# One more fold of the odd rows of a sequence DFT: half-length products for seven of eight sequences

## The chip, the cores and the metric

One core of a Trainium2 chip. The metric is the time of one execution in device microseconds (us). The kernel before the change takes 1992.16 us, the median of 4 runs that share their rounds with the changed kernel (1991.02 to 1994.47). "PE" is TensorE, "DVE" VectorE, "ACT" ScalarE, "POOL" GpSimd.

## The reference

```python
def _attn_ref(x):                       # x: 8 x 3008 x 256, fp32
    X = np.fft.fft(x, axis=1)
    X = np.fft.fft(X, axis=2)
    return X.real.astype(np.float32)

def _moe_ref(x, w_in, w_out):           # x: 24064 x 256; w_in 256 x 2048; w_out 2048 x 256
    h = x @ w_in
    r = np.maximum(h, 0.0)
    return ((r * r) @ w_out).astype(np.float32)
```

The output of the first part, reshaped to 24064 x 256, is the input of the second.

## The kernel before

The DFT over the 3008 rows of a sequence is done as products with cosine and sine tables. Symmetries cut it down: row n is folded with S - n and S/2 +- n, so 753 rows remain (S = 3008), and these fall into classes. Class 3 holds the 376 odd n; it is by far the longest product. The classes are cut into tiles of at most 128 rows: class 0 has one of 95 rows, class 1 one of 94, class 2 two of 128 and 60, class 3 three of 128, 128 and 120.

The feature DFT is merged into the input weights (`G1`, `G2`), and the two weight products run over 6 blocks of 251 output rows with 8 steps each, 48 steps a sequence. While PE works on sequence b, the engines fold sequence b + 1 and PE does its DFT in between; small "pieces" of that work are released by `between()`, twice a step, according to a pace.

```python
def group(kp, which):                      # one of 4 groups of a sequence: even or odd k, cosine or sine part
    ...
    def product(ps, c):
        ts = [t for t in range(NT) if TILES[t][0] == c]
        for t in ts:
            rows = TILES[t][3]
            w = we[t] if b is None else folded[b, t, which % 2]
            w = w[0:rows, kp]
            ...
            nc.tensor.matmul(ps, w, tab[0:rows, kp, PLACE[t]:PLACE[t] + NC[kp][c]],
                             start=t == ts[0], stop=t == ts[-1])

    def even_n():                          # classes 0, 1, 2: 95, 94, then 128 and 60 rows
        ...
        for c, at, nk in ((0, 0, n2), (1, n2, n2), (2, 2 * n2, n1)):
            product(st["ps"][:, at:at + nk], c)
        nc.scalar.copy(a[:, 0:n2], st["ps"][:, 0:n2])
    ...
    def odd_n():                           # class 3: 128, 128, 120 rows, 377 or 376 columns
        st["odd"] = psd.tile([P, 512], F32, name="pd", tag="d")[0:n, 0:n0]
        product(st["odd"], 3)
```

```python
def between():
    nonlocal spent
    if i < 2 * NJ:                         # NJ = 8 steps a block
        return
    spent -= pace
    while side and spent <= 0:
        t, f = side.pop(0)                 # t: weight of the piece, f: emits its instructions
        f()
        spent += t
```

The stationary operand of a DFT product is the folded data (up to 128 rows x 128 columns); the table streams past it. Each fp32 product in the source appears in the trace as two passes, each with a weight load.

## Time and profile before

| | before |
|---|---|
| median, this comparison | 1992.16 us |
| PE busy | 1957.8 us, 98% |
| DVE / ACT / POOL busy | 70% / 45% / 58% |
| distance of one DFT to the next (steady sequences) | 237.77 us |
| one even-n group, first pass to next product | 1.48 us |
| one odd-n group, first pass to next product | 1.90 us |

A busy engine is read here from the page's shares, the critical path from the chain that ended last, and the cost of a product from the *starts* of passes in the timeline. The recorded length of a pass is longer than what it costs: a pass of 189 columns is recorded with 0.32 us, but the next one starts 0.16 us after it. The prediction shows those lines. The distance of one DFT to the next is read off the chain in order of time, where the first even-n group of each sequence stands:

```profile
467.16 1.28 PE pd L349 x8
...
704.93 1.28 PE pd L349 x8
```

704.93 - 467.16 = 237.77 us. All six steady sequences agree to a few hundredths of a us.

### The profile page before, as it was taken

To read this page: it belongs to the slowest core of one execution; us is meant where nothing else is said; L and a number is where in the kernel's file an instruction comes from. 1 tells how busy PE (TensorE), PEld (TensorE's weight loads), DVE (VectorE), ACT (ScalarE), POOL (GpSimd) and SP (SyncE) were. 2 spreads that over 40 slices of the span, in tenths; PEclk is the share of its full clock that TensorE was granted. 3 is DMA by queue.
4 is the path that set the end of the run, shared out by engine and by line. 5 is a ranking of instruction groups with operands and counts; after the bars stand their busy time and mean duration, and the time that the engine had idled before them with its cause. 6 is when DMAs were issued, how large, how long until landed. Compare 5 with 4: busy or idle time off the path is not lost.

```text
span 1991.9 us, 27283 instructions
## 1 busy us (share of the span) xinstructions
PE 1957.8 (98%) x9104; PEld 1701.1 (85%) x9104; DVE 1391.3 (70%) x3492; ACT 896.2 (45%) x973; POOL 1158.8 (58%) x1695
## 2 busy tenths in 40 slices
PE   6999999999999999999999999999999999999998
PEld 3788888888888888888888888888888888888887
DVE  7889867776578765787558875677756876555554
ACT  1654444444444444444344443444444444445443
POOL 0037646666566655666557665666656675566664
PEclk8999999999999999999999999999999999999999
DMA  6331101110011111111011110121002100100100
GB/s 190 110 39 47 38 11 37 47 27 22 18 46 32 40 19 27 27 41 39 11 32 32 39 30 11 32 51 29 22 11 52 32 11 16 32 11 11 22 11 21
DMA packets 144687, 68.49 MB, mean 34 GB/s; under 512 B 128440, under 2 KB 135547, under 8 KB 144546
## 3 DMA queue, kind: packets, MB, share of 16 engines
q1 hardware_dynamic: 143470, 66.24, 14.1%
q8 instruction: 71, 1.16, 0.2%
q14 instruction: 70, 0.57, 0.1%
q10 hardware_dynamic: 1076, 0.52, 0.1%
HBM read 42.03 MB, written 24.68 MB: 33 GB/s over the span
## 4 chain that ended last, share of the span: by engine, by line
PE 94%; DVE 2%; DMA 1%; ACT 1%; SPq 0%; issue 0%; DVEq 0%; ACTq 0%
PE ph L412 16%; PE ph L413 16%; PE mA L465 16%; PE mC L465 16%; PE mB L465 16%; PE mD L465 8%; PE pd L349 5%; DMA xt<-in_x_dram 1%; DMA raw<-in_moe_w_in_dram 1%; DVE he L415 0%; DVE g L418 0%; ACT g L427 0%; ACT g L428 0%; SPq L163 0%; DVE g L417 0%
## 5 line engine op out<-in xcount | busy, mean ns | idle before, releaser
L427 ACT ACTIVATE g<-g 128x1004 f32<-128x1004 f32 (+1 forms) x384 | 399.6, 1041 | 894.3 <-DVE g L418 511.1
L415 DVE SCALAR_TENSOR_TENSOR he<-Et,gE,ph 128x251 f32<-128x251 f32 (+1 forms) x768 | 361.8, 471 | 476.6 <-PE ph L413 475.1
L435 POOL TENSOR_TENSOR s<-g 128x251 f32<-128x251 f32 (+1 forms) x376 | 248.9, 662 | 739.3 <-ACT g L428 668.1
L412 PE MATMUL ph<-Pt,G 128*128 128x251 f32 (+1 forms) x1536 | 453.4, 376 | 4.5 <-ACT G L237 3.4
L413 PE MATMUL ph<-Qt,G 127*128 127x251 f32 (+1 forms) x1536 | 451.3, 374 | 0.2 <-DVE Qt L362 0.2
L428 ACT ACTIVATE g<-g 128x1004 f32<-128x1004 f32 (+1 forms) x384 | 399.3, 1040 | 12.1
L465 PE MATMUL mC<-s,wsum 128*128 128x251 f32 (+1 forms) x1504 | 381.3, 374 | 0.0
L465 PE MATMUL mA<-g,wout 128*128 128x251 f32 (+1 forms) x1504 | 381.0, 375 | 0.0
L417 DVE TENSOR_TENSOR g<-he,ph 128x251 f32<-128x251 f32 (+1 forms) x768 | 320.6, 417 | 55.6 <-POOL s L437 0.5
L412 PEld LDWEIGHTS ph<-Pt,G 128*128 128x128 f32 x1536 | 287.2, 189 | 48.7 <-ACT G L237 4.0
L413 PEld LDWEIGHTS ph<-Qt,G 127*128 127x128 f32 x1536 | 291.1, 190 | 36.4 <-DVE Qt L362 0.6
L465 PEld LDWEIGHTS mA<-g,wout 128*128 128x128 f32 x1504 | 282.5, 189 | 41.7 <-issue 2.9
L465 PEld LDWEIGHTS mC<-s,wsum 128*128 128x128 f32 x1504 | 285.5, 190 | 34.5
L418 DVE TENSOR_TENSOR g<-he,ph 128x251 f32<-128x251 f32 (+1 forms) x768 | 314.2, 409 | 0.0
L436 POOL TENSOR_TENSOR s<-s,g 128x251 f32<-128x251 f32 (+1 forms) x376 | 282.0, 750 | 29.4
L437 POOL TENSOR_TENSOR s<-g 128x251 f32<-128x251 f32 (+1 forms) x376 | 291.4, 775 | 0.0
L438 POOL TENSOR_TENSOR s<-g,s 128x251 f32<-128x251 f32 (+1 forms) x376 | 246.0, 654 | 0.0
L465 PE MATMUL mB<-g,wsum 128*128 128x251 f32 (+1 forms) x752 | 220.5, 374 | 0.0
L465 PE MATMUL mD<-s,wout 128*128 128x251 f32 (+1 forms) x752 | 220.3, 374 | 0.0
L465 PE MATMUL mB<-s,wout 128*128 128x251 f32 (+1 forms) x752 | 219.9, 374 | 0.0
L465 PEld LDWEIGHTS mB<-g,wsum 128*128 128x128 f32 x752 | 142.6, 190 | 17.4
L465 PEld LDWEIGHTS mD<-s,wout 128*128 128x128 f32 x752 | 141.9, 189 | 17.7
(85 smaller groups left out, 1264.3 us busy)
## 6 DMA issues: line engine op xcount, KB each, us to landing
out_dram<-os SPq DMA_DIRECT2D x376, 56.0 KB
xt<-in_x_dram SPq DMA_DIRECT2D x24, 512.0 KB
xt<-in_x_dram SPq DMA_DIRECT2D x16, 384.0 KB
Et<-e_dram SPq DMA_DIRECT2D x7, 752.5 KB
out_dram<-os SPq DMA_DIRECT2D x288, 6.8 KB
raw<-in_moe_w_in_dram SPq DMA_DIRECT2D x16, 256.0 KB
raw<-in_moe_w_out_dram SPq DMA_DIRECT2D x16, 256.0 KB
xt<-in_x_dram SPq DMA_DIRECT2D x8, 480.0 KB
```

The source lines that it names most:

```text
L412: nc.tensor.matmul(hP, G1[:, fs], pt[:, ks], start=True, stop=True)
L413: nc.tensor.matmul(hQ, G2[:, fs], qt[:, ks], start=True, stop=True)
L415: nc.vector.scalar_tensor_tensor(out=t, in0=et[:, ks], scalar=gE[:, fc:fc + 1], in1=hP, op0=ALU.mult, op1=ALU.add)
L417: tt(out=g[:, h, 0, 0:n], in0=t, in1=hQ, op=ALU.add)
L418: tt(out=g[:, h, 1, 0:n][:, ::-1], in0=t, in1=hQ, op=ALU.subtract)
L427: act(v, v, AF.Relu)
L428: act(v, v, AF.Square)
L435: gt(out=s1, in0=g21, in1=g22, op=ALU.add)
L436: gt(out=s2, in0=s1, in1=g11, op=ALU.subtract)
L437: gt(out=s3, in0=g11, in1=g21, op=ALU.subtract)
L438: gt(out=s4, in0=g12, in1=s2, op=ALU.subtract)
L465: nc.tensor.matmul(acc[nm][:, i, 0:n], w, v[:, 0:n], start=j == 0 and i == 0, stop=j == NJ - 1, skip_group_check=True)
```

## The change

The 376 odd rows are folded once more, n with S/4 - n, into 188 rows for each of two data sets. For even k both sets multiply the same table, one its even and one its odd columns, and each yields every second output column (`ps[:, part:n0:2]`). For odd k one set multiplies the cosine table and the other the sine table, and the output columns are sums and differences of the two (`join_odd`). Per odd-n group PE then streams 4 products of 189 or 188 columns instead of 3 of 377 or 376. For each of the two new tiles the fold needs rows in reverse order (a lane shuffle on DVE), two more additions, a rotation by a twiddle factor per row (ACT and DVE), and tables whose even and odd columns are sorted apart, done once on ACT. Also, the preparation of sequence 1 begins eight steps earlier at half pace. Sequence 0 keeps the old form.

```diff
             def odd_n():
-                st["odd"] = psd.tile([P, 512], F32, name="pd", tag="d")[0:n, 0:n0]
-                product(st["odd"], 3)
+                ps = psd.tile([P, 512], F32, name="pd", tag="d")[0:n]
+                st["odd"] = ps[:, 0:n0]
+                if b == 0 or b is None and kp:
+                    return product(ps[:, 0:n0], 3)
+                nq = (n0 + 2) // 2 if kp else (n0 + 1) // 2
+                for part in range(2):
+                    ...                    # tab, o, to = where this part reads and writes
+                    for i, (rows, pair) in enumerate(((P, (ODD0, ODD0 + 1)), (REST, (ODD0 + 2, NT)))):
+                        nc.tensor.matmul(to, folded[b, pair[other]][0:rows, kp, PART[which]][:, 0:n],
+                                         columns(tab, ODD0 + i, o)[0:rows], start=i == 0, stop=i == 1)
+                if kp:
+                    st["cos"] = hp.tile([P, nq], F32, name="oc", tag="oc", bufs=1)[0:n]
+                    nc.scalar.copy(st["cos"], ps[:, 0:nq])
+                    st["sin"] = ps[:, nq:2 * nq]
...                                        # fold pieces of the odd tiles
+        def f_even():
+            v, w, a = st["v"][rows, 0], st["w"][rows, 0], st["f0"][rows]
+            tt(out=v, in0=a, in1=w, op=ALU.add)
+            tt(out=w, in0=a, in1=w, op=ALU.subtract)
+            sine(spare("f1", "f1"), st["w"], (0, 1))
+            sine(spare("f2", "f0"), st["v"], (1, 0))
...
-        return [(0.7, f_s), (0.7, f_d), (0.5, f_sc), (0.4, f_dc), (0.6, f_p), (0.6, f_q)]
+        ops = [(0.7, f_s), (0.7, f_d), (0.6, f_sc), (0.4, f_dc), (0.5, f_p), (0.5, f_q)]
...
+        return ops + [(0.7, f_turn), (0.9, f_even), (1.0, f_odd)]
...
-        if i < 2 * NJ:
+        if i < NJ:
             return
-        spent -= pace
+        spent -= pace / 2 if i < 2 * NJ else pace
```

Here `P` is 128 and `REST` is 60: 188 = 128 + 60.

More of the change, by code (lines that the diff above doesn't have):

```diff
@@ L112 @@
     fp = ctx.enter_context(tc.tile_pool(name="fp", bufs=2))
-    wp = ctx.enter_context(tc.tile_pool(name="wp", bufs=NT))
+    wp = ctx.enter_context(tc.tile_pool(name="wp", bufs=NT + 1))
     pq = ctx.enter_context(tc.tile_pool(name="pq", bufs=2))
@@ L129 @@
     xt = {}
-    def load_x(b, t):
-        _, r0, step, rows = TILES[t]
+    ODD0 = NT - 3
+    HALF = S // 16
+    REST = HALF - P
+    ODD = [[(0, 0, P)],
+           [(p, 2 * HALF - p - R, R) for p in range(0, P, R)],
+           [(0, P, H // 2)] + [(H // 2 + p, 2 * HALF - P - p - R, R) for p in range(0, H // 2, R)]]
+    assert H == P and REST <= H // 2 and TILES[ODD0][0] == 3 and TILES[ODD0 + 1][1] == TILES[ODD0][1] + P
+    def load_x(b, t):
+        c, r0, step, rows = TILES[t]
+        if b and c == 3:
+            xt[b, t] = xp.tile([P, 4, D], F32, name="xt", tag="x")
+            for p, first, count in ODD[t - ODD0]:
+                nc.sync.dma_start(out=xt[b, t][p:p + count], in_=x[b, S // 8 + 1 + first:S // 8 + 1 + first + count])
+            return
         while rows % 15 and rows % 16 and r0 + step * rows < NROW:
@@ L263, with make_turn, part_table, columns @@
     PQE = {}
+    PART = (slice(0, H + 1), slice(H + 1, D))
+    REVERSE = list(range(R - 1, -1, -1))
+    turn = const.tile([P, 3, 2], F32, name="turn")
+    def make_turn():
+        for i in range(2):
+            for a, tab in enumerate((cosT, sinT, sinT)):
+                nc.scalar.mul(turn[:, a, i:i + 1], tab[:, 1, PLACE[ODD0 + i]:PLACE[ODD0 + i] + 1], -1.0 if a == 2 else 1.0)
+    def part_table(tab, t):
+        nk = NC[0][3]
+        v = tab[:, 0, PLACE[t]:PLACE[t] + nk]
+        a = op.tile([P, nk], F32, name="tp", tag="os")
+        nc.scalar.copy(a, v)
+        nc.scalar.copy(v[:, 0:(nk + 1) // 2], a[:, 0::2])
+        nc.scalar.copy(v[:, (nk + 1) // 2:], a[:, 1::2])
+    def columns(tab, t, part):
+        nk, at = NC[0][3], PLACE[t]
+        if t == NT - 1:
+            return tab[:, 0, at + part:at + nk:2]
+        nq = (nk + 1) // 2
+        return tab[:, 0, at + part * nq:at + (nk if part else nq)]
     NE = B - 1
@@ L266 @@
     e_dram = dp.tile([NE, NKT], F32, name="e_dram")
-    e_rows = const.tile([NE, NKT], F32, name="e_rows")
     def load_column(t):
@@ L285, in fold @@
     def fold(b, t):
-        r = slice(0, TILES[t][3])
+        odd = b > 0 and t >= ODD0
+        r = slice(0, P if odd else TILES[t][3])
         st = {}
@@ L312, in f_dc, with w_of @@
             tt(out=new(fp, "dc", [P, 2, H - 1])[r], in0=d[r, :, 1:H], in1=d[r, :, D - 1:H:-1], op=ALU.subtract)
+        def w_of(t):
+            if (b, t) not in folded:
+                folded[b, t] = wp.tile([P, 2, D], F32, name="w", tag="w")
+            return folded[b, t]
         def f_p():
-            sc, wP = st["sc"], new(wp, "wP", [P, 2, H + 1])
+            sc, w = st["sc"], w_of(t)
             for kp in range(2):
-                tt(out=wP[r, kp], in0=sc[r, 0], in1=sc[r, 1], op=ALU.subtract if kp else ALU.add)
@@ L318, in f_p @@
-            folded[b, t, 0] = wP
+                tt(out=w[r, kp, PART[0]], in0=sc[r, 0], in1=sc[r, 1], op=ALU.subtract if kp else ALU.add)
         def f_q():
-            dc, wQ = st["dc"], new(wp, "wQ", [P, 2, H - 1])
+            dc, w = st["dc"], w_of(t)
             for kp in range(2):
-                tt(out=wQ[r, kp], in0=dc[r, 0], in1=dc[r, 1], op=ALU.add if kp else ALU.subtract)
-            folded[b, t, 1] = wQ
-        return [(0.7, f_s), (0.7, f_d), (0.5, f_sc), (0.4, f_dc), (0.6, f_p), (0.6, f_q)]
+                tt(out=w[r, kp, PART[1]], in0=dc[r, 0], in1=dc[r, 1], op=ALU.add if kp else ALU.subtract)
@@ new lines, in fold, with f_turn @@
+        ops = [(0.7, f_s), (0.7, f_d), (0.6, f_sc), (0.4, f_dc), (0.5, f_p), (0.5, f_q)]
+        if not odd or t == ODD0:
+            return ops
+        i = t - ODD0 - 1
+        rows = slice(0, TILES[ODD0 + i][3] if i == 0 else REST)
+        def f_turn():
+            w = w_of(t)
+            if i == 0:
+                st["v"], st["w"] = w_of(ODD0), w
+                nc.vector.stream_shuffle(w, w, REVERSE)
+            else:
+                st["v"], st["w"] = w, w_of(NT)
+                nc.vector.stream_shuffle(st["w"][0:H // 2], w[H // 2:P], REVERSE)
+            spare("f0", "f0")
+            nc.scalar.copy(st["f0"][rows], st["v"][rows, 0])
@@ new lines, in spare, with sine @@
+        def spare(nm, tag):
+            st[nm] = fp.tile([P, D], F32, name=nm, tag=tag, bufs=1)
+            return st[nm]
+        def sine(to, src, signs):
+            for part, a in zip(PART, signs):
+                nc.scalar.mul(to[rows, part], src[rows, 1, part], turn[rows, 1 + a, i:i + 1])
+        def f_even():
[4 more added lines that the diff above has]
+            sine(spare("f2", "f0"), st["v"], (1, 0))
@@ L328, in dft_ops, with f_odd @@
+        def f_odd():
+            for nm, u in (("f1", "v"), ("f2", "w")):
+                u = st[u][rows, 1]
+                nc.vector.scalar_tensor_tensor(out=u, in0=u, scalar=turn[rows, 0, i:i + 1], in1=st[nm][rows],
+                                               op0=ALU.mult, op1=ALU.add)
+        return ops + [(0.7, f_turn), (0.9, f_even), (1.0, f_odd)]
     def dft_ops(b):
@@ L345, in product @@
                     rows = TILES[t][3]
-                    w = we[t] if b is None else folded[b, t, which % 2]
-                    w = w[0:rows, kp]
+                    w = (we[t] if b is None else folded[b, t][:, :, PART[which % 2]])[0:rows, kp]
                     w = w[:, H:H + 1].to_broadcast([rows, n]) if which == 2 and b is not None else w[:, 0:n]
@@ L378, in odd_n @@
             def odd_n():
-                st["odd"] = psd.tile([P, 512], F32, name="pd", tag="d")[0:n, 0:n0]
-                product(st["odd"], 3)
+                ps = psd.tile([P, 512], F32, name="pd", tag="d")[0:n]
[5 more added lines that the diff above has]
+                    if kp:
+                        tab, o = (cosT, sinT)[part], 0
+                        to = ps[:, part * nq:part * nq + nq]
+                        other = part != which
+                    else:
+                        tab, o = (cosT, sinT)[which % 2], part
+                        to = ps[:, part:n0:2]
+                        other = part != which
+                    if b is None:
+                        for t in range(ODD0, NT):
+                            rows, at = TILES[t][3], PLACE[t]
+                            nc.tensor.matmul(to, we[t][0:rows, kp], columns(tab, t, part)[0:rows],
+                                             start=t == ODD0, stop=t == NT - 1)
+                        continue
+                    for i, (rows, pair) in enumerate(((P, (ODD0, ODD0 + 1)), (REST, (ODD0 + 2, NT)))):
+                        nc.tensor.matmul(to, folded[b, pair[other]][0:rows, kp, PART[which]][:, 0:n],
+                                         columns(tab, ODD0 + i, o)[0:rows], start=i == 0, stop=i == 1)
@@ new lines, in odd_n, with join_odd @@
+                if kp:
+                    st["cos"] = hp.tile([P, nq], F32, name="oc", tag="oc", bufs=1)[0:n]
+                    nc.scalar.copy(st["cos"], ps[:, 0:nq])
+                    st["sin"] = ps[:, nq:2 * nq]
+            def join_odd():
+                a, ps = st["cos"], st["sin"]
+                nq = a.shape[-1]
+                st["odd"] = o = hp.tile([P, NC[1][3]], F32, name="do", tag="do", bufs=1)[0:n, 0:n0]
+                tt(out=o[:, 0::2], in0=a[:, 0:nq - 1], in1=ps[:, 0:nq - 1], op=ALU.add)
+                if which == 1:
+                    tt(out=o[:, 1::2], in0=ps[:, 1:nq], in1=a[:, 1:nq], op=ALU.subtract)
+                else:
+                    tt(out=o[:, 1::2], in0=a[:, 1:nq], in1=ps[:, 1:nq], op=ALU.subtract)
@@ L382, in join_1 @@
             def join_1():
-                dst = e_rows if b is None else PQE[b][which]
+                dst = PQE[1][2][0:n] if b is None else PQE[b][which]
                 nh = S // 8
@@ L386, in join_1 @@
                      st["odd"])
-            return [(0.5, even_n), (0.5, join_4), (0.7, join_2), (0.0, odd_n), (1.2, join_1)]
+            ops = [(0.1, even_n), (0.5, join_4), (0.7, join_2), (0.1, odd_n), (1.1, join_1)]
+            if b and kp:
+                ops.insert(4, (0.7, join_odd))
+            return ops
         ops = [] if b is None else [(0.0, start)]
@@ L394, in dft_ops @@
         if b is None:
-            ops.append((0.0, lambda: nc.sync.dma_start(out=e_dram[:, :], in_=e_rows)))
+            ops.append((0.0, lambda: nc.sync.dma_start(out=e_dram[:, :], in_=PQE[1][2][0:NE])))
         return ops
@@ L630 @@
                 load_column(i - NJ)
+            if i == NJ:
+                make_turn()
+            if NJ <= i < NJ + 4:
+                part_table((cosT, sinT)[i % 2], ODD0 + (i - NJ) // 2)
             if i % per == 0:
@@ L633 @@
                 side = ahead(b + 1) if b + 1 < B else []
-                spent, pace = 0.0, sum(t for t, _ in side) / (2 * (per - (0 if i else 2 * NJ)) - 6)
+                spent, pace = 0.0, sum(t for t, _ in side) / (2 * per - 6 - (0 if i else 3 * NJ))
             g = front(b, k0, n, j, between)
```

## The prediction

> **What bounds the kernel now.** I read the page's busy shares first, then the chain of waits, then one stretch in the middle of the run, then single products in the timeline. The shares and the chain:
>
> ```profile
> PE 1957.8 (98%) x9104; PEld 1701.1 (85%) x9104; DVE 1391.3 (70%) x3492; ACT 896.2 (45%) x973; POOL 1158.8 (58%) x1695
> ...
> PE 94%; DVE 2%; DMA 1%; ACT 1%; SPq 0%; issue 0%; DVEq 0%; ACTq 0%
> PE ph L412 16%; PE ph L413 16%; PE mA L465 16%; PE mC L465 16%; PE mB L465 16%; PE mD L465 8%; PE pd L349 5%; DMA xt<-in_x_dram 1%; DMA raw<-in_moe_w_in_dram 1%; DVE he L415 0%; DVE g L418 0%; ACT g L427 0%; ACT g L428 0%; SPq L163 0%; DVE g L417 0%
> ```
>
> TensorE sets the end. The change touches only the sequence DFT, "PE pd L349", 5% of the chain (some 100 us), and of it only the odd-n products. The second view is the busy time of 704 to 942 us, one whole later sequence:
>
> ```profile
> 704.00:942.00 238.00, 238.00 (x1115) 208.53 (x1114) 167.50 (x418) 107.57 (x113) 148.88 (x216) 1.00 0.13 30
> ```
>
> The columns after the length are PE, PE weight loads, DVE, ACT, POOL, then the clock. PE has no gap and the full clock; DVE is busy for 167.5 of 238 us, ACT for 107.6, POOL for 148.9. So a later sequence is worth what its TensorE instructions take, and DVE has 70 us to spare in it.
>
> But a busy PE is not a PE at its peak, so I looked at starts. Each fp32 product in the source is two passes in the trace, each with its own weight load. Odd-n of one group (three products of 377 columns) on the PE, then the weight loads of an even-n group:
>
> ```profile
> 477.83 2.07 PE L349 MATMUL pd<-cosT,wP 128*128 128x377 f32 x6
> 479.73 0.59 PE L465 MATMUL mA<-g,wout 128*128 128x251 f32 x2
> ```
>
> ```profile
> 466.79 0.85 PEld L349 LDWEIGHTS pd<-cosT,wP 95*128 95x128 f32 x6
> 467.86 0.29 PEld L349 LDWEIGHTS pd<-cosT,wP 60*128 60x128 f32 x2 [0.22 <-issue]
> 468.37 0.51 PEld L465 LDWEIGHTS mA<-g,wout 128*128 128x128 f32 x3 [0.22 <-issue]
> ```
>
> (Start, length, engine, line, output and inputs, rows*columns, passes.) Six passes of 377 columns start at 477.83 and the next product at 479.73: 1.90 us, 317 ns a pass, 0.84 ns a column, nothing lost. The even-n group is different: the loads stop for 0.22 us before the 60-row tile and for 0.22 us again when 128-row weights come back. Everywhere else loads are pulled under the running pass.
>
> What a switch costs, from the same stretch: the last 128-row pass of 189 columns starts at 467.61 and, at 0.84 ns a column, needs 0.16, so it is through at 467.77. The first 60-row weights start loading only at 467.86. A load takes 0.11 (the 95-row passes follow each other at 0.11), so the pass starts at 467.97. The lost time is 467.97 - 467.77 = 0.20 us. At the way out the two 60-row passes end at 467.97 + 2 x 0.16 = 468.29, the loads restart at 468.37, and the second pass of mA starts at 468.69 in the timeline, so the first ran from 468.48: 0.19 to 0.20 us again. One excursion into 60 rows costs 0.40 us.
>
> Is that the switch, or an instruction stream that runs dry after short passes? The one-column stage answers, where passes are long:
>
> ```profile
> 291.83 0.19 PEld L413 LDWEIGHTS ph<-Qt,G 127*128 127x128 f32 x1
> 292.35 0.10 PEld L349 LDWEIGHTS pd<-cosT,we 128*7 128x7 f32 x2 [0.32 <-issue]
> ...
> 294.35 0.30 PEld L412 LDWEIGHTS ph<-Pt,G 128*128 128x128 f32 x2 [0.63 <-DVE g L418]
> ```
>
> Here weights of 7 columns replace weights of 128. The load is again not hidden going in and coming back, with passes of 377 columns around it that leave ample time to issue. So I take the shape of the array, not the issue rate.
>
> **What the Trainium skill says.** "TensorEngine Tiling (Array Packing)", Key Properties: changing the tiling mode drains the TensorE; its modes are 128, 64 or 32 rows. Sixty rows fit the 64-row mode; 94 and 95 do not. The trace agrees: no gap at 95, 94, 120 or 128 rows, 0.20 us at 60. "TensorE: Matmul & The Clock Gate", LDWEIGHTS: a load's time depends on its columns, not its rows, by columns / 1.2, so 107 ns for 128; the trace has 0.11 us. "SBUF — State Buffer", Door 1, says that any non-contiguous PSUM access significantly slows matmuls. The final transposes, which write every second PSUM word, disagree: three passes of 128 columns from 1983.53 end at 1984.02, 0.49 us for two steps and a last pass of 0.27, so 0.11 a step, the rate of a load.
>
> **The change part by part.**
>
> Removed from TensorE: in each of 4 groups of 7 sequences (28 groups), three products of 377 (376) columns over 128, 128 and 120 rows: 6 passes, 1.90 us. Total 28 x 1.90 = 53.3 us.
>
> Added: four products of 189 (188) columns, 8 passes of 0.159 us = 1.27 us. On columns alone the saving would be 0.63 us a group, 17.7 us in all, 0.9%. But the folded rows number 188, cut as 128 + 60, and the loop runs part 0 (128 rows, 60 rows), then part 1 (128, 60). The instruction order of the changed kernel, compared with the old, confirms this alternation. That is two excursions a group: 2 x 0.40 = 0.80 us. A new odd-n group takes 1.27 + 0.80 = 2.07 us against 1.90: **0.17 us more**. Over 28 groups +4.6 us.
>
> The one-column stage: one of its two odd products becomes 12 passes of 189 columns in place of 6 of 377, 1.91 against 1.90. Its strided table reads are of one tile only. Nothing.
>
> Added on DVE per later sequence, estimates from rows of like shape: two lane shuffles of 512 columns (the 32x32 transposes of 448 take 0.638, so 0.7 each), four additions of 256 columns at some 0.5, four scalar-tensor operations at 0.47 (L415), four joins of 188 columns at 0.345 (the L366 row of that size): 1.4 + 2.0 + 1.9 + 1.4 = 6.7 us. DVE goes from 167.5 to 174 of 238. Hidden. On ACT: two copies of 256 columns (0.35), eight scalings of about 128 (0.25), two copies of 189 (0.3), 3.3 us, from 107.6 to 111. Hidden. They are spread by the pace and the back products run two steps behind the front, so a relu that is delayed by 2 us is not seen. Loads grow by 8 rows a sequence; DMA share is 0.13. The four sorted tables and six scale columns are some 6 us of ACT once, in a stage where ACT is half idle.
>
> Moved: the preparation of sequence 1 starts at step 8 rather than 16, at half pace. DVE is busy for about 3.4 to 3.8 of the 4.7 us of steps 8 to 15, and gets about 1 us more: tight, but it fits, while steps 16 to 30 are relieved a little. PE lost about 2 us there (steps of 4.8 to 5.8 us in place of 4.67). I put this at -1 to +3 us, no net in the middle.
>
> Sum: 1992.5 + 4.6 = 1997.
>
> **The rivals.**
>
> Columns rule. If the gaps around 60 rows came from something that the new order does not repeat, the full 17.7 us come back and the time is 1975. For it: the page's own word for the gap is "issue", not a drain. Against it: the gap sits at each 60-row tile, and at the 7-column one, and nowhere else. About 8%.
>
> Strided PSUM writes. In the even-k groups (14 of 28) the two parts write every second word of one bank. If such passes ran at half rate, 14 x 8 x 0.16 = 18 us more, 2015. For it the skill's sentence, against it the transposes. About 6%.
>
> A new wait on DVE or ACT. The new chain goes DVE, ACT, DVE, ACT, DVE in strict queues, between operations that feed PE. If each of 14 chains held PE for 0.3 us it would be +4 us; if steps 8 to 15 become DVE-bound, +4 once. For it: DVE's tight steps there; against it: 30% of DVE idle later, and pieces that come at least half a step apart. This makes the upper side of the range.
>
> **Range and chances.** The centre is the drain sum, 1997. Small waits and the earlier start give -4 to +7, so 1990 to 2005 holds it 8 times in 10; the other two are mostly the first two rivals, 1975 and 2015, and both of these are still within 2% (1952.6 to 2032.3). Chances: faster 0.02, same 0.95, slower 0.03.
>
> **What would show it right or wrong.** In the changed kernel an odd-n group, first pass to next product, should take 2.05 to 2.1 us; its weight loads should show two stops before 60-row tiles and two after, 0.2 us each. A period of a later sequence (237.8 us, from the starts of a DFT group at 467.16 and 704.93 in the chain) should grow to about 238.4. If the group takes 1.3 us, the columns rule; if even-k groups take a microsecond more than odd-k ones, it is the stride. If PE shows idle before L537 (the front product) with DVE as releaser in later sequences, the wait has come. A group of 1.9 us or less with the total well below 1990 would make this prediction wrong.

## The result, and the profile after

The changed kernel takes 1998.97 us (median of 4, 1998.19 to 2000.5) against 1992.16. The ratio is 1.0034, 95% interval 1.0016 to 1.0051: slower by a third of a per cent. All outputs are right. Ratios in this document are the mean time of one kernel's fast runs over the mean time of the other's fast runs of the same rounds, so they are not quite the ratio of the medians.

The busy shares and the chain of the page of the changed kernel:

```profile
PE 1962.6 (98%) x9166; PEld 1701.9 (85%) x9166; DVE 1462.2 (73%) x3604; ACT 926.2 (46%) x1075; POOL 1166.8 (58%) x1695
...
PE 91%; DVE 6%; ACT 1%; issue 0%; DMA 0%; SPq 0%; DVEq 0%
PE ph L537 16%; PE mA L590 16%; PE ph L538 16%; PE mC L590 15%; PE mB L590 15%; PE mD L590 8%; PE pd L486 3%; PE pd L435 2%; DVE he L540 1%; DVE g L542 1%; DVE g L543 1%; DVE w L366 1%; DVE dc L356 0%; ACT g L552 0%; ACT g L553 0%
```

PE did not get less busy although it streams fewer columns. And DVE has come into the chain, with 6% in place of 2%. (That share says through which engine the chain runs, not how much time was lost.) The distance of one DFT to the next, from the chain in order of time:

```profile
475.52 1.28 PE pd L435 x8
482.52 1.86 PE pd L486 x8
...
714.33 1.28 PE pd L435 x8
```

714.33 - 475.52 = 238.81 us, 1.04 us more than before (1.06 on the mean of the steady sequences). (L435 is the even-n group, L486 the new odd-n one. The 1.86 of the chain runs from the recorded end of the product before, 482.52, to the recorded end of the last pass, 484.38; from the first pass to the next product it is more, as follows.) The weight loads of one odd-n group, in the timeline:

```profile
482.15 0.40 PEld L486 LDWEIGHTS pd<-cosT,w 128*128 128x128 f32 x2
482.77 0.29 PEld L486 LDWEIGHTS pd<-cosT,w 60*128 60x128 f32 x2 [0.22 <-issue]
483.29 0.30 PEld L486 LDWEIGHTS pd<-cosT,w 128*128 128x128 f32 x2 [0.22 <-issue]
483.80 0.29 PEld L486 LDWEIGHTS pd<-cosT,w 60*128 60x128 f32 x2 [0.22 <-issue]
484.31 0.30 PEld L590 LDWEIGHTS mA<-g,wout 128*128 128x128 f32 x2 [0.22 <-issue]
```

The loads stop four times for 0.22 us: into 60 rows, out, in, out. The first pass starts at 482.36 in the PE timeline, and the next product can start when its load is done, at 484.31 + 0.11 = 484.42. The group takes 2.06 us, of which 8 x 0.159 = 1.27 us are columns.

The second difference lies in the eighth step of each of the six steady sequences. Both engines there, in the timeline of the changed kernel:

```profile
353.82 0.59 PE L538 MATMUL ph<-Qt,G 127*128 127x251 f32 x2
...
354.54 0.41 DVE L543 TENSOR_TENSOR g<-he,ph 128x251 f32<-128x251 f32 x1
354.87 0.87 DVE L356 TENSOR_TENSOR dc<-fd 94x254 f32<-94x254 f32 x1
355.66 1.53 DVE L366 TENSOR_TENSOR w<-sc 94x129 f32<-94x129 f32 x2
357.11 0.46 DVE L540 SCALAR_TENSOR_TENSOR he<-Et,gE,ph 128x251 f32<-128x251 f32 x1
...
358.40 0.69 PE L537 MATMUL ph<-Pt,G 128*128 128x251 f32 x2 [0.17 <-DVE g L543]
```

Two fold pieces run back to back in one half step: 357.11 - 354.87 = 2.24 us of DVE. Its next work on the front product (L540), whose operand PE finished at 354.41, starts only at 357.11. The buffers of the front product come free late and PE waits. In the starts of the front products this step is 5.11 us long where the other steps without a DFT group are 4.67. The waits of PE over the whole run (who waited for whom: us in total, times, longest) for the front product on DVE, before, after, and in the run e5_pace that follows below:

```profile
PE ph L412 <- DVE g L418: 0.9, 1, 0.9
PE ph L537 <- DVE g L543: 2.7, 9, 0.7
PE ph L537 <- DVE g L543: 0.6, 1, 0.6
```

The page's own averages hide both effects: PE is 98% busy before and after.

### The profile page after: what moved, and what is told of

Read it like the earlier page. It is cut to its first block, busy times and chain, and to the rows that moved or that the text cites. A ratio compares the mean times of both kernels' runs of the same rounds, so it can differ in the third digit from the quotient of the medians.

```text
span 1997.9 us, 27668 instructions
## 1 busy us (share of the span) xinstructions
PE 1962.6 (98%) x9166; PEld 1701.9 (85%) x9166; DVE 1462.2 (73%) x3604; ACT 926.2 (46%) x1075; POOL 1166.8 (58%) x1695
## 4 chain that ended last, share of the span: by engine, by line
PE 91%; DVE 6%; ACT 1%; issue 0%; DMA 0%; SPq 0%; DVEq 0%
PE ph L537 16%; PE mA L590 16%; PE ph L538 16%; PE mC L590 15%; PE mB L590 15%; PE mD L590 8%; PE pd L486 3%; PE pd L435 2%; DVE he L540 1%; DVE g L542 1%; DVE g L543 1%; DVE w L366 1%; DVE dc L356 0%; ACT g L552 0%; ACT g L553 0%
## 5 line engine op out<-in xcount | busy, mean ns | idle before, releaser
L540 DVE SCALAR_TENSOR_TENSOR he<-Et,gE,ph 128x251 f32<-128x251 f32 (+1 forms) x768 | 361.4, 471 | 405.3 <-PE ph L538 402.9
L537 PE MATMUL ph<-Pt,G 128*128 128x251 f32 (+1 forms) x1536 | 455.1, 377 | 6.1 <-ACT G L255 3.4
L537 PEld LDWEIGHTS ph<-Pt,G 128*128 128x128 f32 x1536 | 286.0, 189 | 51.6 <-DVE g L543 7.3
L563 POOL TENSOR_TENSOR s<-g,s 128x251 f32<-128x251 f32 (+1 forms) x376 | 258.4, 687 | 0.0
```

Source lines behind the costliest of these rows:

```text
L537: nc.tensor.matmul(hP, G1[:, fs], pt[:, ks], start=True, stop=True)
L540: nc.vector.scalar_tensor_tensor(out=t, in0=et[:, ks], scalar=gE[:, fc:fc + 1], in1=hP, op0=ALU.mult, op1=ALU.add)
L563: gt(out=s4, in0=g12, in1=s2, op=ALU.subtract)
```

## The experiments

Theory A, from the prediction: an excursion of the array into 60 rows costs 0.40 us, whatever surrounds it, and two of them per group eat the 0.63 us that a group saves. Rival B: short passes let the instruction issue run dry (the profile calls the gap "issue"). Rival C: it is not the size of the tile but a row count that is no multiple of 32. Theory D concerns the eighth step. The first four runs share one chip and their rounds, the next four another set; e9 came last, on the chip of the second set. Each ratio is to the kernel before in the same rounds (medians 1991.95 to 1992.16 us); the changed kernel was not run again in them.

| run | what | median us | ratio to before (95%) | DFT to DFT, us |
|---|---|---|---|---|
| before | | 1992.16 | 1 | 237.77 |
| after | the change | 1998.97 | 1.0034 (1.0016 to 1.0051) | 238.81 |
| e1_pair | order 128, 128, 60, 60 | 1989.34 | 0.9990 (0.9975 to 1.0004) | 237.28 |
| e2_rows64 | 64 rows in place of 60 | 1999.17 | 1.0038 (1.0021 to 1.0054) | 238.82 |
| e3_rows96 | 96 rows in place of 60 | 1978.22 | 0.9935 (0.9920 to 0.9950) | 235.72 |
| e4_before96 | kernel before, 96 rows in even n | 1979.75 | 0.9942 (0.9927 to 0.9957) | 236.22 |
| e5_pace | other pace weights | 1996.98 | 1.0023 (1.0010 to 1.0035) | 238.39 |
| e6_late | no earlier start | 2000.41 | 1.0046 (1.0032 to 1.0059) | 238.82 |
| e7_unsorted | tables not sorted | 2001.27 | 1.0045 (1.0032 to 1.0057) | 239.06 |
| e8_all96 | 96 rows in odd and even n | 1966.95 | 0.9873 (0.9859 to 0.9886) | 234.17 |
| e9_best | e8 and e5 | 1962.35 | 0.9849 (0.9836 to 0.9861) | 233.84 |

### e1_pair: half the excursions, same work

```diff
-                for part in range(2):
+                for i, part in ((0, 0), (0, 1), (1, 0), (1, 1)):
...
-                                         columns(tab, ODD0 + i, o)[0:rows], start=i == 0, stop=i == 1)
+                                     columns(tab, ODD0 + i, o)[0:rows], start=i == part == 0, stop=i == 1,
+                                     skip_group_check=True)
```

> The changed kernel with the order of the four odd-n products of a later sequence altered from 128, 60, 128, 60 rows to 128, 128, 60, 60 (same products, same columns, correct result). Theory A (each excursion of the array into 60 rows costs 0.40 us): one excursion per group in place of two, so a group takes 1.66 us in place of 2.06, and the kernel 28 x 0.40 = 11.2 us less than the changed one, 1988 us. Rival B (short passes run the instruction issue dry, whatever their rows): group stays at 2.06 us, kernel at 1999.

Measured: 1989.34 us, 9.6 us under the changed kernel. The distance falls by 238.81 - 237.28 = 1.53 us for four groups, 0.38 us per excursion removed. The weight loads of a group:

```profile
480.45 0.72 PEld L486 LDWEIGHTS pd<-cosT,w 128*128 128x128 f32 x4
481.40 0.61 PEld L486 LDWEIGHTS pd<-cosT,w 60*128 60x128 f32 x4 [0.22 <-issue]
482.23 0.72 PEld L591 LDWEIGHTS mA<-g,wout 128*128 128x128 f32 x4 [0.22 <-issue]
```

One stop in, one stop out. There are as many short passes as before, four of them now consecutive 60-row ones, and nothing stops between them. That speaks for A and against B.

### e2_rows64: a multiple of 32, still half the array

```diff
+    PAD = 64
+    tabR = [sinT[0:PAD, 1, PLACE[ODD0 + a]:PLACE[ODD0 + a] + NC[0][3]] for a in range(2)]   # a table region that is free by then
...
+            nc.vector.memset(a, 0.0)
+            nc.scalar.copy(a[0:REST], v[0:REST])
...
-                    for i, (rows, pair) in enumerate(((P, (ODD0, ODD0 + 1)), (REST, (ODD0 + 2, NT)))):
+                    for i, (rows, pair) in enumerate(((P, (ODD0, ODD0 + 1)), (PAD, (ODD0 + 2, NT)))):
...                                        # the PAD-row product reads tabR
```

> The changed kernel with the 60-row products run over 64 rows, the four added rows of the table being zero (correct result). Theory A (what costs is the 64-row mode of the array): 64 rows are still that mode, group stays 2.06 us, kernel 1999 +- 2. Rival C (an odd number of rows, not a multiple of 32, is what stops the loads): group falls to 1.27 us, kernel to 1977. Rival B (issue): 1999, no difference.

Measured: 1999.17 us and 238.82 us, nothing changed, and the same four stops:

```profile
484.06 0.40 PEld L495 LDWEIGHTS pd<-cosT,w 128*128 128x128 f32 x2
484.68 0.29 PEld L495 LDWEIGHTS pd<-sinT,w 64*128 64x128 f32 x2 [0.22 <-issue]
485.19 0.30 PEld L495 LDWEIGHTS pd<-cosT,w 128*128 128x128 f32 x2 [0.22 <-issue]
485.71 0.29 PEld L495 LDWEIGHTS pd<-sinT,w 64*128 64x128 f32 x2 [0.22 <-issue]
```

Rival C is out (94, 95 and 120 rows, no multiples of 32 either, have no stop in the kernel before). It also shows that the extra table copy, which e3 shares, costs nothing visible.

### e3_rows96: no excursion

As e2, with `PAD = 96` and one more line, since the data rows beyond 64 must hold finite numbers:

```diff
+                nc.vector.memset(st["w"][H // 2:PAD], 0.0)
```

> The same with 96 rows, 36 added rows of the table zero (correct result). Theory A: no switch of mode, no excursion: group 8 x 0.159 = 1.27 us, 28 x 0.79 = 22 us less than the changed kernel, 1977 us. Rival B (issue runs dry on short passes): still 2.06 us and 1999. Rival C as theory A.

Measured: 1978.22 us, 20.8 us under the changed kernel and 0.65% under the one before.

```profile
479.18 0.35 PEld L496 LDWEIGHTS pd<-sinT,w 96*128 96x128 f32 x2
479.50 0.35 PEld L496 LDWEIGHTS pd<-cosT,w 128*128 128x128 f32 x2
479.82 0.35 PEld L496 LDWEIGHTS pd<-sinT,w 96*128 96x128 f32 x2
480.14 0.77 PEld L600 LDWEIGHTS mA<-g,wout 128*128 128x128 f32 x4
```

The loads follow each other without a stop, the group takes 1.28 us in the chain, and the distance is 3.09 us shorter: 0.39 us for each of eight excursions. Rival B would have shown no change: the passes are as short as before and as many, and over more rows. A multiplication by 36 rows of zeros makes the kernel faster.

### e4_before96: the same cost in the kernel before

The even-n groups of the old kernel have a 60-row tile too.

```diff
-    TILES = class_tiles(S)
+    REAL = [rows for *_, rows in class_tiles(S)]
+    TILES = [(c, r0, step, 96 if rows == 60 else rows) for c, r0, step, rows in class_tiles(S)]
...
+            if rows != REAL[t]:
+                nc.gpsimd.memset(tab[0:96, :, PLACE[t]:PLACE[t] + NC[0][c]], 0.0)
+                rows = REAL[t]
```

> The kernel BEFORE the change with its only 60-row tile (in the even-n groups) run over 96 rows, added table rows zero (correct result). Theory A: each of 36 even-n groups loses its one excursion, 1.48 us to 1.08; 36 x 0.40 = 14.4 us less, 1978 us. Rival B: even group stays 1.48 us, 1992.

Measured: 1979.75 us, 12.3 us less than before; the distance is 1.55 us shorter for four excursions, 0.39 us each. That is some 2 us less than expected; e8 below shows why. The even-n group in the weight loads has no stop any more:

```profile
481.77 1.17 PEld L353 LDWEIGHTS pd<-cosT,wP 95*128 95x128 f32 x8
482.91 0.35 PEld L416 LDWEIGHTS ph<-Pt,G 128*128 128x128 f32 x2
```

So the cost was in the kernel all along, paid by the 36 even-n groups (in full by 28 of them, see e8), and the change multiplied it rather than introduced it: 36 excursions became 36 + 28 x 2 = 92.

### e5_pace: the eighth step

```diff
-        ops = [(0.7, f_s), (0.7, f_d), (0.6, f_sc), (0.4, f_dc), (0.5, f_p), (0.5, f_q)]
+        ops = [(0.8, f_s), (1.0, f_d), (1.1, f_sc), (0.7, f_dc), (1.2, f_p), (1.0, f_q)]
...
-        return ops + [(0.7, f_turn), (0.9, f_even), (1.0, f_odd)]
+        return ops + [(0.7, f_turn), (1.6, f_even), (1.5, f_odd)]
```

> The changed kernel with other pace weights for the pieces of the fold, close to their measured DVE time (0.8, 1.0, 1.1, 0.7, 1.2, 1.0 and 0.7, 1.6, 1.5 in place of 0.7, 0.7, 0.6, 0.4, 0.5, 0.5 and 0.7, 0.9, 1.0); same instructions. Theory D: the 0.43 us that PE loses in the eighth step of each of six sequences comes from two pieces (2.4 us of DVE) released in one half step; spread apart it vanishes: period 238.83 to 238.40, 2 to 3 us less than the changed kernel. Rival: DVE lacks time on average, the loss moves to another step, period stays 238.83.

Measured: 1996.98 us, and the distance from the chain:

```profile
493.21 1.28 PE pd L435 x8
...
731.60 1.28 PE pd L435 x8
```

731.60 - 493.21 = 238.39 us, 0.42 less than the changed kernel, as theory D has it. The total is 2.0 us lower; its interval overlaps that of the changed kernel, so it is the distance that decides. No instruction was added or removed. The stall came from weights that were too small for the pieces (0.4 + 0.5 for 2.24 us of DVE), not from a lack of DVE time. (All weights of the fold were changed at once, so that these two alone would do is not shown.)

### e6_late: without the earlier start

```diff
-        if i < NJ:
+        if i < 2 * NJ:
             return
-        spent -= pace / 2 if i < 2 * NJ else pace
+        spent -= pace
```

(The pace is again the sum of the weights over the slots from step 16 on.)

> The changed kernel with the earlier start undone: sequence 1 is prepared from step 16 on at full pace, as before the change. Theory: the earlier start relieved steps 16 to 30 about as much as it burdened steps 8 to 15, so undoing it moves the time by less than 3 us, more likely up since the new chain then has to fit in the same steps: 1999 to 2002. Rival: the early start is what costs: 1996 or less.

Measured: 2000.41 us; the steady distance is unchanged at 238.82. From the first front product of sequence 0 to that of sequence 1 the traces have 270.6 us before, 272.2 after and 273.9 here. The earlier start saves 1.7 us of the changed kernel. Against the changed kernel the totals do not differ clearly (1.0046 and 1.0034 with overlapping intervals).

### e7_unsorted: is the sorting worth it?

```diff
-        if t == NT - 1:
-            return tab[:, 0, at + part:at + nk:2]
-        nq = (nk + 1) // 2
-        return tab[:, 0, at + part * nq:at + (nk if part else nq)]
+        return tab[:, 0, at + part:at + nk:2]
...
-            if NJ <= i < NJ + 4:
-                part_table((cosT, sinT)[i % 2], ODD0 + (i - NJ) // 2)
```

> The changed kernel without the sorting of the tables: all odd-n products of the later sequences read every second column. Theory F: TensorE streams every second fp32 word as fast as adjacent ones: an odd-n group stays 2.06 us, time 1999 +- 2. Rival G: such reads run at half rate: 28 x 8 x 0.159 = 36 us more, 2034.

Measured: 2001.27 us. An odd-n group of the changed kernel and of this one in their chains:

```profile
482.52 1.86 PE pd L486 x8
```

```profile
481.87 1.92 PE pd L483 x8
```

Reading every second column costs 0.06 us a group, 8 ns a pass; the distance grows by 0.25 us and seven sequences by 1.7 us. Neither "free" nor "half rate": sorting is worth a little. Both theories had the wrong size here, F by less.

### e8_all96 and e9_best: both repairs

e8 is e3 and e4 in one kernel, e9 adds e5.

> The changed kernel with both kinds of 60-row product (odd-n and even-n) run over 96 rows of which 36 have zero table entries (correct result). Theory A: no excursion anywhere; the two savings add: 22 + 14 us less than the changed kernel, 1963 to 1964 us, period 238.83 - 3.10 - 1.55 = 234.2. Rival: the even groups' gap was partly covered by other work, the saving does not add: 1970 or more.

Measured: 1966.95 us, some 3 us above what was expected, and a distance of 234.17, as expected to 0.03 us. The steady part adds exactly. The kept traces show where the missing 3 us lie. From the first front product of one sequence to that of the next, each of the seven stretches is 4.65 us shorter than in the changed kernel, the first one too (272.16 to 267.50), together 32.6 us; the medians differ by 32.0. The expectation counted all 92 excursions, but 8 of them, 3.1 us, bring almost nothing that shows. The six even-n groups of sequence 0 run before the first front product, in a start-up in which PE stands idle for some 20 us anyway; it ends at 52.38 us in the changed kernel and at 52.33 here, and varies from 50.2 to 54.5 over all eleven traces. The two even-n groups with weights of 7 columns gain only 0.09 us each (1.16 to 1.07). The same eight are most of what e4 fell short of: its seven stretches are 10.8 us shorter where 14.4 were expected in all.

> The changed kernel with both remedies: 60-row products run over 96 rows and the pace weights near the measured DVE times (correct result). If they add: the 1967 us of the padded version less the 2 to 3 us of the pace, 1964 to 1965; period of a later sequence 234.18 - 0.43 = 233.75. If the shorter DFT groups bring the next DVE stall instead: 1967.

Measured: 1962.35 us, ratio 0.9849 to before: 1.5% faster than the kernel before and 36.6 us under the changed one. The pace saves 0.33 us a sequence here, a little less than the 0.42 alone, and the stretch of sequence 0 is another 1.3 us shorter (267.50 to 266.22). This is the fastest version measured.

## Why the prediction was right or wrong

The time on record was 1997, the measured median 1998.97, inside the range of 1990 to 2005. The centre counted the excursions alone; what it left out, the stalls on DVE, comes to 2.6 us. Two small slips of the working: 28 x 0.17 is 4.8, not 4.6, and -4 to +7 around 1997 is 1993 to 2004, narrower than the range given. Point by point:

- **The removed and added columns** came out: the passes cost what their columns say where no stop is left (1.28 us a group in e3, 1.27 predicted).
- **The excursion** is confirmed in size and in cause. Predicted 0.40 us, measured 0.38 to 0.39 in e1, e3 and e4. The group was put at 2.07 us and took 2.06, with the four stops foreseen. Rival B is contradicted by e1, e3 and e4, rival C by e2. The first rival of the prediction ("columns rule", 1975 us) is what e3 produces by removing the excursions: 1978.
- **What is shown of the mechanism:** the cost appears at a change between 128 and 60 (or 64) rows, not per short pass, and not at 94, 95, 96 or 120 rows. Between 64 and 94 rows nothing was measured. In the prediction's working, 0.09 of the 0.20 us pass before the load starts (467.77 to 467.86), and the other 0.11 are the load, no longer hidden. That the array drains at the change is what "TensorEngine Tiling (Array Packing)", Key Properties, in the Trainium skill states; the trace shows the stop of the loads that fits it, not the drain itself.
- **The lines of the 7-column stage** need care. Between those that the prediction shows stand others, such as `292.67 0.09 PEld L349 LDWEIGHTS pd<-cosT,we 128*7 128x7 f32 x1 [0.23 <-issue]`: short loads between long passes of one shape leave the loader idle too, and nothing is lost, as the passes still start 0.32 us apart. The switch shows in the starts. The last 128-column pass before it starts at 292.04 and, with 250 columns, is through at 292.25; the 7-column load starts only at 292.35. At the way back the last pass is through at 294.26 and the load starts at 294.35. (The view names DVE there, but that work had ended at 293.78.) So the reading stands, by 0.09 us each way and not by the 0.32 and 0.63 of the view.
- **Strided PSUM writes** cost nothing. Even-k groups write every second word and take 1.86 us in the chain, odd-k groups write adjacent ones and take 1.87; in e3, where no stop could hide a slower pass, it is 1.28 and 1.29.
- **"Hidden" for DVE was the step that failed**, at the scale of 2 to 3 us. Two things were off. The added DVE work was put at 6.7 us a sequence; the stretch of one sequence has 178.5 us against 167.5, so 11.0. Its scalar-tensor operations took 0.74 us where 0.47 was assumed, the 256-column additions 0.73 and 0.80 where 0.5 was. More important, the argument compared averages (30% of DVE idle), while the loss is made in one half step in which two pieces fall together. Six times 0.43 us are 2.6 us, and e5 removes them. The prediction had this as its rival "A new wait on DVE or ACT", and the sign that it named came: PE waits before L537 for DVE. A period was to grow to about 238.4 and grew to 238.83; the difference is this stall.
- **The earlier start** was put at -1 to +3 us with no net; e6 shows that it saves 1.7 us of what the change would otherwise cost in the first sequence. With it, that stretch is 1.5 us longer than before (270.62 to 272.16), of which 0.6 are its four odd-n groups. The other 0.9 us lie in the range given; with the weights of e5 the stretch is 270.57, so they too hang on the pace.
- The sum: 28 groups x 0.16 = 4.5 us, six stalls 2.6 us, 0.9 us in the first sequence, together 8.0, against 6.8 us between the medians. In a steady sequence the sum closes: 4 x 0.16 + 0.43 = 1.07 us against 1.06. The rest is the start-up, which ended 2.1 us earlier in the trace of the changed kernel than in that of the kernel before (52.38 and 54.49), but varies by 4 us over the traces, and with no order that follows the changes. So the agreement of the total to better than 2 us is in part luck. The groups rest on e1 to e4, the stalls on e5.

The windows of one sequence of the changed kernel, from which the 178.5 is read (columns as in the prediction: PE, PE weight loads, DVE, ACT, POOL, clock):

```profile
802.20:1041.00 238.80, 238.63 (x1121) 208.46 (x1120) 178.50 (x433) 110.91 (x125) 150.38 (x216) 1.00 0.11 30
```

Why a fold piece takes so long at times can be seen in the kernel before, where the same operation on 129 columns (L317) has these shortest, median and longest times in ns:

```profile
L317 DVE TENSOR_TENSOR wP<-sc x112: 276/290/817, 9.3 to 1652.3; 128x129 f32<-128x129 f32 x48, 95x129 f32<-95x129 f32 x16, 94x129 f32<-94x129 f32 x16, 60x129 f32<-60x129 f32 x16
```

The Trainium skill, "SBUF — State Buffer", Who interferes with whom, says that a DVE instruction with two SBUF inputs contends with a GpSimd instruction that reads SBUF. The trace agrees: the pair of 1.53 us above (0.77 each) runs while POOL is busy without a gap. Of the 112 operations of this kind in the changed kernel (L366), the 17 during which POOL was idle throughout took 0.28 to 0.30 us; of the 94 with POOL busy for at least half of their time, half took more than 0.6 us, up to 0.82. No run here isolates it.

## What to carry to other kernels

Fewer columns are not less time if the new tiles change the shape of the array: count the switches between row modes in the issue order as well as the columns, and pad a tile of 60 or 64 rows to 96 with zero table rows, or put such tiles next to each other. Look for the cost in the weight loads of the timeline (here a 0.22 us stop at each change of rows), and confirm it by the starts of the passes, because the busy share of PE does not show it. Where side work is released by weights, set them from measured times: a mean idle share of 25 to 30% does not protect against two pieces in one slot.

## What the Trainium skill lacked or had wrong

- "TensorEngine Tiling (Array Packing)", Key Properties: says that a switch of the tiling mode drains the array, but gives no cost and no warning that a lone tile of 60 or 64 rows between 128-row products costs like one. Measured for fp32 with 128 weight columns: 0.38 to 0.40 us per excursion (in and out), the same for 60 and 64 rows, none at 94, 95, 96 and 120.
- The same page, When to Use Tiling, names contractions of up to 64 rows as the case for row tiling and does not say that one such product alone among 128-row products loses. Here 96 rows with zeros were 20.8 us faster over 56 excursions (e3), 12.3 us over 36 (e4). Several small tiles side by side, which the page is about, were not tried.
- "SBUF — State Buffer", Door 1: says that any non-contiguous PSUM access significantly slows matmuls. Writing every second fp32 word took 1.86 us a group, adjacent words 1.87 (1.28 and 1.29 in e3).
- The same section counts fp32 strides of up to 4 elements within a 16-byte line and asks for two hits a line. A moving operand with step 2 (two hits) was not quite free: on average 8 ns more on a pass of 159 ns (e7).
- "TensorE: Matmul & The Clock Gate", Back-to-back issue gap, gives the spacing of products by columns without a case for fp32 (another page counts passes of an fp32 product, but gives no time). Here a fp32 product is two passes, each with its own load, at 0.84 ns a column and pass and never closer than about 0.11 us with 128 weight columns.
